# Attention with a block beside it: three pairs of PSUM banks from step 67, and another order of the units

## The chip, the cores and the metric

The kernel runs on one core of one Trainium2 chip. The metric is the device time of one execution in microseconds. One execution was taken by the hardware profiler; all instruction times below come from it. Engines are called as in the profile: PE (matrix multiply; PEld is its weight load), DVE (vector), ACT (scalar), POOL (GpSimd), and SP, which here only issues DMAs. PSUM, where PE writes its results, has eight banks of 512 fp32 columns in each partition as the kernel divides it.

## The reference

One transformer block on x of shape (1, 2048, 448), fp32: layer norm with a shift and scale from a condition vector c, attention with 16 heads of 28, a gated residual, a second such norm, a mixer MLP with 1792 hidden units, a gated residual.

```python
def _A_ref(x, wqkv, wo):
    B, S, D = x.shape
    H = 16; Dh = D // H
    qkv = (lambda x, *d: x.transpose(*d))((x @ wqkv).reshape(B, S, 3, H, Dh), 2, 0, 3, 1, 4)
    q, k, v = qkv[0], qkv[1], qkv[2]
    scale = Dh ** -0.5
    scores = jnp.einsum("bhqd,bhkd->bhqk", q, k) * scale
    p = _softmax(scores, axis=-1)
    o = jnp.einsum("bhqk,bhkd->bhqd", p, v)
    return (lambda x, *d: x.transpose(*d))(o, 0, 2, 1, 3).reshape(B, S, D) @ wo
...
mod = (_silu(c) @ w_mod).reshape(c.shape[0], 6, 1, -1)
sa, ca, ga, sb, cb, gb = (mod[:, 0], mod[:, 1], mod[:, 2], mod[:, 3], mod[:, 4], mod[:, 5])
h = _layernorm(x, axis=-1) * (1 + ca) + sa
x = x + ga * _A_ref(h, A_wqkv, A_wo)
h = _layernorm(x, axis=-1) * (1 + cb) + sb
x = x + gb * _B_ref(h, B_w1, B_b1, B_w2, B_b2)
```

The softmax needs, for each head and query, the largest score, so that the exponentials don't overflow. The kernel computes these maxima by matmuls of their own.

## The kernel before

**Three phases.** Phase 1 (up to about 182 us) makes q, k and v in 512-token blocks and stores q and k, split in a high and a low part for precision, in DRAM. The attention follows (to about 843 us), then the MLP. The change concerns the attention.

**Units and steps.** The 16 heads form four groups g of four heads; the four heads lie in the four 32-row strips of the PE array, 28 rows of data each and a 29th row that carries, on the side of k, a one and, on the side of q, the negated maximum. The queries form four blocks qt of 512. A unit is one (g, qt); there are 16, g outermost: (0,0), (0,1), ... (3,3). A unit has 16 steps kt, one for each 128 keys: 256 steps in all, numbered `step = u * NKT + kt`. A step does in this order:

- the scores of its 128 keys for heads 0 and 1 of the group (`hf` 0, array rows 0 to 63), six matmuls (three terms high × high, low × high, high × low for each of two heads) into a tile of two banks (`ps_s2`, two such tiles), L1051; then the same for heads 2 and 3 (`hf` 1, rows 64 to 127);
- after each half one exponential on ACT of the whole two-bank tile (L1059), into SBUF tiles `slot_c` and `slot_d`;
- between the score matmuls three or four **maxima matmuls** (L392), each one strip of 32 rows against 512 keys into one of three single banks (`ps_mx`), each followed by a DVE reduction over the 512 columns (L397) into `mxp`;
- the product of the previous step's exponentials with v (`av`, L1015), in one bank `o`.

So PSUM is three banks `mx`, two times two banks `s` and one `o`.

**The queue of maxima.** A unit needs 64 maxima: four 128-query tiles i, four heads j, four key blocks cch. They must all be done before the unit's scores start. `queue_max` sorts them by g, then by qt; `emit_max` takes the next that fits the half of the array which the scores leave free. `n_maxima` gives 4 and 3 in turn, and few in steps with output-projection work. `count` reloads a key block (`kh`) or query block (`qh`) for the next g as soon as its last reader is issued (`load_hi`, SP). Phase 1 already does some maxima of later groups. `finish_max` at step kt = 10 makes sure that the next unit's are done; `max_fin` and `put` then negate, transpose and send them by four small DMAs into the 29th rows of the unit's q tile. When no maxima are left, `share(1, 3)` gives a third score tile.

**Loads.** `load_k` brings the next group's keys (four chunks of two 256 KB parts) during the last unit of a group, after the step that read the chunk last; `load_q` brings a unit's queries.

**End of a unit.** `unit_end_tasks` spreads over the steps of the next unit: the denominators (L767 to L776, through DRAM), the division on POOL (L781), the split in high and low (L791, L792). A unit whose g isn't the last for its qt stores this to DRAM. The last unit of a qt loads what the others stored (`load_o`) and does the output projection in four tasks `t_wo`, one in each of the steps kt 8 to 11 of the next unit: 12 matmul terms (9 where three groups take part) of 128 rows × 448 columns into an `mx` bank, an ACT copy (L812) and a POOL addition. So projections run in units 12, 13, 14 and 15. The last group of the last block is left to the MLP phase.

## Time and profile before

| | us |
|---|---|
| median of 3 runs | 1141.04 (1140.98 to 1141.12) |
| the profiled execution | 1142.17 |
| its span, first to last instruction | 1140.4 |
| PE busy | 1127.8 |
| DVE busy | 831.6 |
| ACT busy | 683.4 |
| attention, first exponential to the start of the last step's | 184.15 to 842.27 |
| granted PE clock, mean | 0.998 |

Here are a few rows of the view by line (line, engine, operation, output and inputs with partitions × elements, count; busy time and mean duration of one in ns; idle time of the engine just before them and what ended it):

```profile
L1051 PE MATMUL s<-slot_b,slot_a 32*128 32x512 f32 x3072 | 376.0, 420 | 1.6 <-ACT full L812 0.7 <-ACT v L376 0.6 <-ACT slot_c L1059 0.3
L1059 ACT ACTIVATE slot_c<-s 128x1024 f32<-128x1024 f32 x341 | 339.5, 1022 | 77.1 <-PE s L1051 76.7
L1051 PEld LDWEIGHTS s<-slot_b,slot_a 32*128 32x128 f32 x3072 | 211.9, 183 | 250.2 <-ACT slot_c L1059 147.9 <-ACT slot_d L1059 74.8 <-issue 9.1
L392 PE MATMUL mx<-kh,qh 32*128 32x512 f32 x899 | 290.1, 469 | 0.3
```

Busy time is the union of what runs: 3072 score matmuls of 420 ns fill 376.0 us because up to four run side by side in their strips. In the views by stretch of time a row gives the stretch, its length, then for each engine its busy time with the count of instructions, then the granted clock, the DMA engines' mean busy share and GB/s. In the timeline a row gives start, duration, engine, line, operation, output and inputs, the count of merged instructions, and in brackets the idle time before and what ended it. A matmul's duration reaches to its modelled end.

### The profile page before, as it was taken

To read this page: it belongs to the slowest core of one execution; us is meant where nothing else is said; L and a number is where in the kernel's file an instruction comes from. 1 tells how busy PE (TensorE), PEld (TensorE's weight loads), DVE (VectorE), ACT (ScalarE), POOL (GpSimd) and SP (SyncE) were. 2 spreads that over 40 slices of the span, in tenths; PEclk is the share of its full clock that TensorE was granted. 3 is DMA by queue.
4 is the path that set the end of the run, shared out by engine and by line. 5 is a ranking of instruction groups with operands and counts; after the bars stand their busy time and mean duration, and the time that the engine had idled before them with its cause. 6 is when DMAs were issued, how large, how long until landed. Compare 5 with 4: busy or idle time off the path is not lost.

```text
span 1140.4 us, 20798 instructions
## 1 busy us (share of the span) xinstructions
PE 1127.8 (99%) x8380; PEld 678.4 (59%) x8380; DVE 831.6 (73%) x1487; ACT 683.4 (60%) x839; POOL 245.9 (22%) x277
## 2 busy tenths in 40 slices
PE   8999999999999999999999999999999999999998
PEld 6767765444444444444444444545468888888887
DVE  6868787999999999999999977493648853444322
ACT  4655757878878887888788877586762321211110
POOL 2634431211011011101110121214514503123000
PEclk9999999999999999999999999999999999999999
DMA  9543345121222111222211212022113100000000
GB/s 299 194 144 125 111 160 156 38 62 44 67 84 75 53 45 39 76 76 66 66 30 58 89 63 76 10 85 85 53 55 87 43 34 1 1 33 1 33 1 33
DMA packets 50296, 81.12 MB, mean 71 GB/s; under 512 B 12308, under 2 KB 21592, under 8 KB 50200
## 3 DMA queue, kind: packets, MB, share of 16 engines
q1 hardware_dynamic: 44536, 74.83, 20.8%
q0 software_dynamic: 5376, 4.51, 1.5%
q8 instruction: 66, 1.08, 0.4%
q10 hardware_dynamic: 288, 0.46, 0.1%
q14 instruction: 30, 0.25, 0.1%
HBM read 53.11 MB, written 26.35 MB: 70 GB/s over the span
## 4 chain that ended last, share of the span: by engine, by line
PE 95%; DVE 1%; ACT 1%; DMA 1%; issue 1%; POOL 0%; DVEq 0%; ACTq 0%; POOLq 0%
PE s L1051 27%; PE o L1015 22%; PE mx L317 16%; PE pa L339 7%; PE mx L392 7%; PE s L1112 4%; PE s L1113 4%; PE s L1111 4%; PE pa L317 3%; DMA slot_c<-in_w_mod_dram 1%; PE o L240 1%; PE mx L240 1%; PE o L547 0%; ACT slot_c L1059 0%; DMA acc<-in_A_x_dram 0%
## 5 line engine op out<-in xcount | busy, mean ns | idle before, releaser
L397 DVE TENSOR_REDUCE mxp<-mx 128x1 f32<-128x512 f32 x919 | 580.3, 684 | 102.0 <-PE mx L392 95.2
L1059 ACT ACTIVATE slot_c<-s 128x1024 f32<-128x1024 f32 x341 | 339.5, 1022 | 77.1 <-PE s L1051 76.7
L1051 PE MATMUL s<-slot_b,slot_a 32*128 32x512 f32 x3072 | 376.0, 420 | 1.6 <-ACT full L812 0.7
L1051 PEld LDWEIGHTS s<-slot_b,slot_a 32*128 32x128 f32 x3072 | 211.9, 183 | 250.2 <-ACT slot_c L1059 147.9
L392 PE MATMUL mx<-kh,qh 32*128 32x512 f32 x899 | 290.1, 469 | 0.3
L1015 PE MATMUL o<-slot_c,v 128*32 128x512 f32 x1364 | 270.5, 605 | 0.5 <-ACT osb L983 0.4
L1059 ACT ACTIVATE slot_d<-s 128x1024 f32<-128x1024 f32 x171 | 174.7, 1022 | 38.4 <-PE s L1051 38.1
L1015 PE MATMUL o<-slot_d,v 128*32 128x512 f32 x684 | 179.9, 605 | 0.0
L1095 ACT ACTIVATE full<-mx,b_col 128x512 f32<-128x512 f32 x56 | 38.5, 688 | 192.2 <-PE mx L317 180.1
L392 PEld LDWEIGHTS mx<-kh,qh 32*128 32x128 f32 x899 | 115.3, 182 | 7.5 <-DVE mxp L397 1.9
L1098 DVE CAST hi<-full 128x512 fp32r<-128x512 f32 x56 | 25.2, 450 | 129.3 <-ACT full L1095 129.3
L1015 PEld LDWEIGHTS o<-slot_c,v 128*32 128x32 f32 x1364 | 38.0, 108 | 54.9 <-issue 50.1
L317 PE MATMUL mx<-y,slot_a 128*128 128x512 f32 x160 | 60.6, 395 | 0.0
L767 POOL DMA_DIRECT2D den<-osb x16 | 11.4, 716 | 192.5 <-ACT osb L983 192.5
L405 ACT ACTIVATE slot_d<-mx 128x512 f32<-128x512 f32 x48 | 27.0, 597 | 40.0 <-PE mx L392 39.8
L1099 DVE TENSOR_TENSOR lo<-full,hi 128x512 fp32r<-128x512 f32 x56 | 44.1, 788 | 5.6 <-PE mx L240 0.5
L317 PE MATMUL mx<-y,slot_c 128*128 128x512 f32 x152 | 47.5, 396 | 0.1
L1113 PE MATMUL s<-slot_v,lo 128*128 128x448 f32 x128 | 46.7, 365 | 0.0
L1111 PE MATMUL s<-slot_v,hi 128*128 128x448 f32 x128 | 46.6, 364 | 0.0
L1015 PEld LDWEIGHTS o<-slot_d,v 128*32 128x32 f32 x684 | 24.6, 108 | 27.3 <-issue 25.1
L774 POOL DMA_DIRECT2D drec<-den x16 | 9.3, 578 | 145.1 <-DVE den L772 145.1
L317 PE MATMUL mx<-y,slot_v 128*128 128x512 f32 x112 | 39.2, 396 | 0.0
(223 smaller groups left out, 1484.3 us busy)
## 6 DMA issues: line engine op xcount, KB each, us to landing
d<-lo SPq DMA_DIRECT2D x32, 256.0 KB
slot_b<-d SPq DMA_DIRECT2D x32, 256.0 KB
slot_a<-d SPq DMA_DIRECT2D x32, 256.0 KB
d<-hi SPq DMA_DIRECT2D x20, 256.0 KB
osb<-drec POOLq DMA_DIRECT2D x16, 256.0 KB, 5.2
out_dram<-xn SPq DMA_DIRECT2D x16, 224.0 KB
slot_v<-in_w_mod_dram SPq DMA_DIRECT2D x4, 784.0 KB
raw<-in_B_w_dram SPq DMA_DIRECT2D x14, 224.0 KB
```

Source lines behind the costliest of these rows:

```text
L317: pe.matmul(p, a, b, start=(i == 0), stop=(i == len(terms) - 1))
L339: pe.matmul(p, *ts[i], start=(i == 0), stop=(i == len(ts) - 1))
L392: pe.matmul(m, qh_sb[(g, qt)][js, i * 128 : (i + 1) * 128], k[js, :], start=True, stop=True)
L397: dve.tensor_reduce(out=mxp[(g, qt)][:, i, j, cch : cch + 1], in_=m, op=ALU.max, axis=AX.X)
L1015: pe.matmul(o[32 * j : 32 * j + 32, :], v_sb[kt // 4][:, kt % 4, 4 * g + j, :], p[j // 2][:, j % 2, :], start=(kt == 0), stop=(kt == NKT - 1),
L1051: pe.matmul(s2[:, jj, :], ks[rows_, kp, kc], qs[rows_, qp, :], start=(term == 0), stop=(term == 2))
L1059: act.activation(pt[hf], s2, AF.Exp, scale=SCALE)
L1095: act.activation(gf, p, AF.Gelu_apprx_tanh, bias=b1_col[:, i : i + 1])
L1099: dve.tensor_tensor(out=glo, in0=gf, in1=f(ghi), op=ALU.subtract)
L1111: pe.matmul(pp, ghi[:, ts], w_hi, start=(m == 0), stop=False)
L1112: pe.matmul(pp, ghi[:, ts], w_lo, start=False, stop=False)
L1113: pe.matmul(pp, glo[:, ts], w_hi, start=False, stop=(m == NFT - 1))
```

## The change

Four things change in the attention.

- **Order of units.** The first four units stay, (0,0) to (0,3). The others run block by block: (1,0), (2,0), (3,0), (1,1) and so on. From unit 4 on each unit has another group than the next, so keys are loaded during each of units 3 to 14, and the maxima's key blocks follow the order of the queue. Query blocks for the maxima have four slots by unit number. Projections now run in units 7, 10 and 13 (12 terms, kt 10 to 13) and 15 (9 terms, kt 8 to 11); their loads start four steps later, except for unit 15.
- **Banks.** As soon as three maxima per step (eight in a projection step) are enough up to the deadline of every unit (`room`; this is so from step 67), `share(1, 0)` leaves one single bank, and the six others form three pairs, `pairs`. In a step the first half of the scores takes `pairs[0]`, the second `pairs[1]`, two maxima `pairs[2]`; then `pairs[1]` and `pairs[2]` change places. When no maxima are left the three pairs rotate among the scores.
- **Maxima.** Each step has a single (`emit_one`) after the first half's matmuls, in the strips of the second half, and two (`emit_two`) of adjacent heads with one reduction over [128, 2, 512] after the second half, in the strips of the first half. On odd steps the halves change order. In a projection step five more are issued after the fifth term: two pairs and a single; the projection writes into one of the pairs.
- **Deadline.** `finish_max` moves from kt 10 to kt 12.

```diff
+UNITS = [(0, qt) for qt in range(NB)] + [(g, qt) for qt in range(NB) for g in range(1, NG)]
+UNIT_NO = {unit: u for u, unit in enumerate(UNITS)}
...
+    def ps_pair(i):
+        return psp[0].tile([128, 2, 512], F32, tag=f"pair{i}", name=nm("pair"), bufs=1)
...
-    def mm_acc(p, terms):
-        for i, (a, b) in enumerate(terms):
-            pe.matmul(p, a, b, start=(i == 0), stop=(i == len(terms) - 1))
+    def mm_acc(p, terms, done=0, mid=None):
+        for i in range(done, len(terms)):
+            if i == 5 and mid:
+                mid()
+            pe.matmul(p, *terms[i], start=(i == 0), stop=(i == len(terms) - 1))
...
-        tg = ("kh" if kind else "qh") + str(b)
+        tg = f"kh{b}" if kind else f"qh{UNIT_NO[(g, b)] % 4}"
...
-        mxq.sort(key=lambda m: (m[:2] != (0, 0), -m[0] if phase1[0] else m[0], m[1:]))
+        mxq.sort(key=lambda m: (m[:2] != (0, 0), -m[0], m[1:]) if phase1[0] else (UNIT_NO[m[:2]], m[2:]))
...
+        if not phase1[0]:
+            for cch in cchs:
+                run = runs[cch]
+                run[0][1] -= 1
+                if run[0][1] == 0:
+                    run.pop(0)
+                    if run:
+                        load_hi(1, run[0][0], cch)
...
+    def load_next_q(u):
+        if u + 4 < len(UNITS):
+            load_hi(0, *UNITS[u + 4])
...
+    def take(half):
+        fits = [x for x, m in enumerate(mxq[:32]) if m[4] // 2 == half]
+        alone = [x for x in fits if mxq[x][:4] + (mxq[x][4] ^ 1,) not in mxq]
+        return mxq.pop((alone or fits or [0])[0])
+
+    def emit_two(half, t):
+        for x, m in enumerate(mxq[:32]):
+            if m[4] == 2 * half and m[:4] + (m[4] + 1,) in mxq[:40]:
+                g, qt, cch, i, j = m
+                mxq.remove(m)
+                mxq.remove(m[:4] + (j + 1,))
+                for y in range(2):
+                    max_mm(g, qt, i, j + y, kh_sb[(g, cch)], lambda: t[:, y, :])
+                dve.tensor_reduce(out=mxp[(g, qt)][:, i, j : j + 2, cch], in_=t, op=ALU.max, axis=AX.X)
+                count(g, qt, [cch, cch])
+                return
+        two = [take(half) for _ in range(min(2, len(mxq)))]
+        for y, (g, qt, cch, i, j) in enumerate(two):
+            max_mm(g, qt, i, j, kh_sb[(g, cch)], lambda: t[:, y, :])
+        for y, (g, qt, cch, i, j) in enumerate(two):
+            dve.tensor_reduce(out=mxp[(g, qt)][:, i, j, cch : cch + 1], in_=t[:, y, :], op=ALU.max, axis=AX.X)
+            count(g, qt, [cch])
+
+    def emit_one(half):
+        if mxq:
+            m = take(half)
+            max_one(*m)
+            count(*m[:2], [m[2]])
...
-                p = ps_mx()
+                p, spare = wo_banks()
...
-        d_rec, d_split = (4, 8) if staged else (1, 4) if u == NU - 1 else (2, 5)
+        d_rec, d_split, d_wo = (4, 8, 0) if staged else (1, 4, 7) if u == NU - 1 else (2, 5, 7) if u == NU - 2 else (2, 5, 9)
...
-            tasks.append((0, lambda: load_o(qt)))
+            tasks.append((0 if u == NU - 2 else 4, lambda: load_o(qt)))
...
+    def room(s_):
+        need = 0
+        for u in range(s_ // NKT, NU):
+            need += left.get(UNITS[u], 64)
+            if need > sum(8 if is_wo(x) else 3 for x in range(s_, finish_step(u))):
+                return False
+        return True
+
+    def finish_step(u):
+        return NKT * u - 4
+
+    def wo_banks():
+        if not mxq:
+            return ps_mx(), None
+        first, g_, b_ = pairs
+        t = ps_pair(first)
+        pairs[:] = [g_, b_, first]
+
+        def spare():
+            for x, i in enumerate((g_, b_)):
+                if mxq:
+                    emit_two(x, ps_pair(i))
+            emit_one(0)
+
+        return t[:, 0, :], spare
...
-            if not (three or mxq or late):
-                three = True
-                share(1, 3)
+            if not pairs and room(step):
+                pairs = [0, 1, 2]
+                share(1, 0)
...
-            for hf in range(2):
-                s2 = ps_s2()
+            halves = (1, 0) if pairs and step % 2 else (0, 1)
+            for x, hf in enumerate(halves):
+                s2 = ps_pair(pairs[x]) if pairs else ps_s2()
...
+                if pairs and x == 0 and not (step and is_wo(step - 1)):
+                    emit_one(halves[1])
+                if x == 1:
                     p_next = p_tile()
                     pt.append(p_next[:, 0:2, :])
-                act.activation(pt[hf], s2, AF.Exp, scale=SCALE)
+                act.activation(pt[x], s2, AF.Exp, scale=SCALE)
+            if mxq and pairs:
+                emit_two(halves[0], ps_pair(pairs[2]))
+                if step and is_wo(step - 1):
+                    emit_one(halves[1])
+                pairs = [pairs[0], pairs[2], pairs[1]]
+            elif pairs:
+                pairs = [pairs[2], pairs[0], pairs[1]]
+            pt = [pt[halves[0]], pt[halves[1]]]
...
-            if qt == NB - 1 and kt % 4 == 3 and g + 1 < NG:
-                load_k(g + 1, kt // 4)
+            if g_next != g and kt % 4 == 3:
+                load_k(g_next, kt // 4)
```

More of the change, by code (lines that the diff above doesn't have):

```diff
@@ L694, in tile_adaln_block @@
     phase1[0] = False
-    for item in deferred:
-        load_hi(*item)
     for g in range(1, NG):
@@ L936, in w2_item @@
         return ld, go
-    NU = NG * NB
+    NU = len(UNITS)
     sched = {}
```

75 lines of the change are left out of this document (33 added, 42 removed).

## The prediction

> **What bounds the kernel now.** I read the page's busy times first, then three views of the attention stage, which the change touches, by themselves: the exponentials counted by stretch, all engines by stretch, and the timeline.
>
> ```profile
> PE 1127.8 (99%) x8380; PEld 678.4 (59%) x8380; DVE 831.6 (73%) x1487; ACT 683.4 (60%) x839; POOL 245.9 (22%) x277
> ```
>
> PE's 99% doesn't say that PE is the limit: up to four 32-row matmuls run beside each other and all count as one busy stretch. So the stage has to be cut into steps. A step makes two exponentials (L1059). Counted by stretch, then all engines in the middle stretch:
>
> ```profile
> 183.00:348.59 165.59, 129.93 (x134) 1.00 0.23 68
> 348.60:790.60 442.00, 327.79 (x338) 1.00 0.19 57
> ...
> 348.60:790.60 442.00, 441.32 (x4084) 205.19 (x4084) 368.00 (x619) 339.75 (x360) 63.89 (x76) 1.00 0.19 57
> ```
>
> 134 exponentials are 67 steps, so step 67 starts its first one at 348.60; 338 more are 169 steps, so step 236 begins at 790.65. These 169 steps, 67 to 235, take **442.05 us** and are all that the change makes different. Twelve of them hold output-projection work.
>
> ```profile
> 270.05 1.94 ACT L1059 ACTIVATE slot_c<-s 128x1024 f32<-128x1024 f32 x2 [0.80 <-PE s L1051]
> ...
> 271.20 0.49 PE L1051 MATMUL s<-slot_b,slot_a 32*128 32x512 f32 x2
> ...
> 271.21 0.51 PE L392 MATMUL mx<-kh,qh 32*128 32x512 f32 x2
> ...
> 271.54 1.01 PE L1051 MATMUL s<-slot_b,slot_a 32*128 32x512 f32 x6
> 271.77 1.89 DVE L397 TENSOR_REDUCE mxp<-mx 128x1 f32<-128x512 f32 x3 [0.20 <-PE mx L392]
> 272.04 0.18 PEld L1051 LDWEIGHTS s<-slot_b,slot_a 32*128 32x128 f32 x2 [0.32 <-ACT slot_c L1059]
> ...
> 272.21 1.03 ACT L1059 ACTIVATE slot_c<-s 128x1024 f32<-128x1024 f32 x1 [0.22 <-PE s L1051]
> ...
> 272.95 1.06 PE L1015 MATMUL o<-slot_c,v 128*32 128x512 f32 x8
> 273.13 1.02 ACT L1059 ACTIVATE slot_d<-s 128x1024 f32<-128x1024 f32 x1
> ...
> 273.94 0.50 PE L1051 MATMUL s<-slot_b,slot_a 32*128 32x512 f32 x2
> ```
>
> This is a step with four maxima, on the timeline. Scores start at 271.20. The second half of them starts only at 272.04, when the exponential begun before (270.05 + 1.94 = 271.99) has freed its two banks. The product with v follows from 272.95 to 273.94 (1.00). So the scores took 1.75 us instead of what a step with three maxima needs:
>
> ```profile
> 278.96 0.49 PE L1051 MATMUL s<-slot_b,slot_a 32*128 32x512 f32 x2
> ...
> 279.76 0.39 PE L392 MATMUL mx<-kh,qh 32*128 32x512 f32 x2
> 279.80 0.40 PE L1051 MATMUL s<-slot_b,slot_a 32*128 32x512 f32 x2
> 280.12 1.06 PE L1015 MATMUL o<-slot_c,v 128*32 128x512 f32 x8
> ```
>
> Here the scores take 1.16 (278.96 to 280.12); with v's product as above a step is **2.16**. The two kinds alternate, 2.74 and 2.16, so 2.45 on average. The bound is a wait in a ring of buffers: scores with two buffers must wait for ACT, while ACT itself has gaps (0.80 and 0.22 above). Without maxima and with a third score buffer it looks like this:
>
> ```profile
> 802.08 0.98 PE L1051 MATMUL s<-slot_b,slot_a 32*128 32x512 f32 x12
> ...
> 802.99 0.62 PE L1015 MATMUL o<-slot_d,v 128*32 128x512 f32 x2
> ...
> 803.09 2.93 ACT L1059 ACTIVATE slot_c<-s 128x1024 f32<-128x1024 f32 x3 [0.21 <-PE s L1051]
> ```
>
> Both halves run together (other rows of the array), 0.91 from first score to v's product, and the first exponential starts 1.01 after the first score.
>
> **The change part by part.** *How many maxima.* The view by line, DVE alone, over the stage:
>
> ```profile
> L397 DVE TENSOR_REDUCE mxp<-mx 128x1 f32<-128x512 f32 x802 | 505.0, 684 | 76.4 <-PE mx L392 69.6 <-PE s L1051 4.5
> ```
>
> 802 maxima; the first 67 steps, unchanged, emit 4 and 3 in turn: 235. The other 567 are just 3 × 169 + 5 × 12, the new code's three per step and five more inside each of the twelve projection steps. So the maxima still end at step 235, as pairs 157 + 36 = 193 reduces and 181 singles. From 236 on all is as before, but one thing below.
>
> *A plain step.* The six banks now turn: the first half's pair waits for the exponential before it; the second half's pair was the maxima's pair of the step before, so **its wait moves from ACT to DVE**; the maxima's pair waits for the step before's second exponential. The price of the new reduce, 128x1024, is in no row. Nearest are two reads of PSUM on DVE:
>
> ```profile
> L1117 DVE TENSOR_TENSOR xn<-s,acc 128x448 f32<-128x448 f32 x16 | 9.0, 617 | 4.3 <-PE s L1113 4.1
> ```
>
> From 448 to 512 elements (617 to 684) an element costs 1.05 ns, so 1024 take 684 + 536 = **1.22 us**. From below: ACT's 1.02 for the same shape; from above: two singles, 1.37. I take 1.22.
>
> Count from a step's first score. The pair's matmuls are the fourth round, done at 1.20 (280.15 − 278.96); the reduce starts 0.05 later (271.72 to 271.77), ends at 2.47, and the next step's second half may start at 2.52. From there 0.91 to v's product (272.04 to 272.95; the same as both halves together) and 1.00 for it: the step after next begins at 4.43, so two steps take 4.43, one 2.22. DVE has other work in this loop: of its 368.00 us in the stretch, 567 maxima at 505.0/802 = 0.63 take 357, and 11 are left, 0.065 per step. It has 2.22 − 1.17 − 0.63 = 0.42 free per step (the pair's 1.22 less the 0.05 by which a single's 0.68 overlaps the next), so I let half of it count: 0.03. **2.25 per plain step.** Does the rest keep up? The second exponential starts at 1.01 + 0.92 (272.21 to 273.13) and ends at 2.95, so 0.70 into the next step, where the pair's matmul wants it at 0.80: covered by 0.1. Single reduces run from 0.55 (matmul 0.50, start 0.05) to 1.18, before the pair's. The single's bank is free by then. Behind the waiting second half stand, in PE's order, the pair's matmuls and v's product, and ACT's second exponential needs it: those are the 0.91 and the 1.01 counted here.
>
> *A projection step* (rows of one with twelve terms):
>
> ```profile
> 722.93 0.88 PE L317 MATMUL mx<-slot_e,slot_a2h 128*128 128x448 f32 x3
> ...
> 725.26 0.36 PE L317 MATMUL mx<-slot_e,lo 128*128 128x448 f32 x1
> ...
> 725.55 0.50 PE L1051 MATMUL s<-slot_b,slot_a 32*128 32x512 f32 x2
> ```
>
> Twelve terms take 2.62, 0.20 each at the same pace. Five maxima after the fifth term cost two changes of tile shape and two rounds: 0.29 (725.26 to 725.55) + 0.34 (271.20 to 271.54) + 0.32 (279.80 to 280.12) − 0.20 = 0.75, so 3.37. DVE reduces pair, pair, single there; the second pair ends at 0.80 + 0.29 + 0.50 + 0.05 + 1.17 + 1.22 = 4.03, and the next step's second half waits for it until 0.71 into that step (4.08 − 3.37). Together 0.71 + 0.91 + 1.00 + 3.37 = **6.0**. Without that wait it is 5.5 (1.16 + 1.00 + 3.37); with the single's reduce, 0.63, waited for as well, 6.6.
>
> *Order of units.* Key chunks (512 KB) are now fetched per unit, eight units more than before, and the 256 KB key blocks for the maxima likewise: some 25 MB more. They are issued on SP after the last reader, 12 steps (27 us) or more before use. In a burst the queue moved 362 GB/s, so 2 MB need about 6 us:
>
> ```profile
> 705.00:707.00 2.00, 2.00 (x24) 1.12 (x21) 1.74 (x3) 1.79 (x3) 0.00 (x0) 1.00 1.02 362
> ```
>
> So a projection's 1.5 MB load, now five steps ahead (11 us), also fits; a unit's 4 MB in 36 us is a third of this rate. Cost 0; without that cover a chunk that waits for those before it in SP's queue would come up to those 6 us late per unit. The other thing on SP is the small row of maxima, four DMAs per unit:
>
> ```profile
> 716.01 2.24 SPq L439 DMA_DIRECT2D slot_b<-full  x4
> ```
>
> A unit's maxima now may end four steps before it starts and not six. For the last unit they do: the row is sent at step 237 and read at 240, three steps of 2.0 us, in which 2.24 of issue and a landing (no row of it here) fit; I keep 1 us for it below. The projections move to units 7, 10 and 13, and the nine-term one to unit 15, past step 236: 4 × 3 × 0.20 = 2.4 saved there.
>
> *Sum.* 157 × 2.25 + 12 × 6.0 = 353.3 + 72.0; and 4 for the change of pools at step 67 (1), the single held by its one bank in the step after each series (3 × 0.6), and the last row of maxima (1). 429.3 against 442.05 is −12.8, with −2.4 **−15.2**. The profiled execution (1142.17, of which the span is 1140.4) would become 1127.0; the median, 1141.04, becomes **1125.8; I say 1126**.
>
> **The rivals.**
>
> *PE is the floor.* The three-maxima step of before needs 2.16 with no wait. If the reduce is near 1.02 us, two steps take 0.20 less, 2.15 each, and projection steps 5.6: 337.6 + 67.2 + 4 = 408.8, −33.2 − 2.4: **1105**. For it: ACT's row; against: DVE's slope.
>
> *The wait on DVE is longer than the one on ACT (slower).* Its place is the second half's first weight load. Each 0.1 us by which the pair's reduce ends later costs 0.05 per step, 7.9 us in all. The forecast's gain is gone at a step of (442.05 + 2.4 − 72 − 4) / 157 = 2.35, a reduce ending 0.2 later than at 2.47. At 0.38 later (a pair of 1.60 us, or one queued behind a stalled cast) a step is 2.44: 383.1 + 76 = 459.1, +17.1 − 2.4: **1156**. For it: DVE's queue is in order; against: the slope of the two rows.
>
> *Score halves don't overlap.* If PE starts matmuls in program order only, the second half comes after the first, and a plain step is six rounds (the first 0.34, the last 0.32 to v's product, 0.91 − 0.34 − 0.32 = 0.25 between): 0.34 + 4 × 0.25 + 0.32 + 1.00 = 2.66, so 157 × 0.41 = 64 more: **1190**. The twelve score matmuls at 802.08 speak against it: in that order, with one round shared, they would take 0.34 + 3 × 0.25 + 0.32 = 1.41 to v's product, and 0.91 was measured. The Trainium skill, TensorE: Matmul & The Clock Gate, section "The mechanism", says that matmuls start and end in program order without reordering; by that rule this rival would hold, and the row differs.
>
> *It doesn't do what it says.* Where two maxima of a pair aren't both in the queue's window, two single reduces follow each other, 0.63 + 0.68 = 1.31 instead of 1.22: 0.04 per step, 6 us: **1132**. So most of what I expect comes from the turning banks, little from the wide operation.
>
> **How the numbers follow.** The forecast (2.19 to 2.30 per step, 1115 to 1135) has 0.60; the floor 0.15; separate reduces 0.06; slower by the wait on DVE 0.12, a smaller form of it that ends near no change 0.05; no overlap 0.02. The bounds: all low, 157 × 2.15 + 12 × 5.5 + 2 = 405.6, gives 1102; all high, the reduce at 1.37 (2.325 per step), 6.6 and 6, gives 450.2 and 1147. The range, **1104 to 1143**, holds the floor and leaves out about half of the high corner and the slower cases. Within 0.2% (2.3 us, about what a measurement of this kernel can tell from no change) 0.07, slower by more 0.14, faster by more 0.79.
>
> **What would show it.** The new reduce at 1.15 to 1.25 us, 193 of them; first exponentials 2.25 apart from step 67 to 235 in place of 2.74 and 2.16; the second half's weight load waiting 0.3 us, now for the reduce and no longer for ACT; projection steps of about 6.0; step 236 some 13 us earlier than at 790.65; no wait of scores for a DMA. Wrong: a reduce above 1.4 us, steps at 2.35 or more, or key chunks waited for at unit starts.

## The result and the profile after

The changed kernel takes **1183.16 us** (median of four runs, 1181.17 to 1185.17) beside 1141.08 of the kernel before on the same chip: a ratio of **1.0367**, 95% interval 1.0348 to 1.0385. The forecast was 1126, the range 1104 to 1143. It is slower, and by more than the slower rival (1156). The profiled execution took 1181.17 with a span of 1179.4.

The page of the changed kernel, its busy time and DMA totals:

```profile
PE 1154.2 (98%) x8380; PEld 690.0 (59%) x8380; DVE 819.1 (69%) x1297; ACT 683.2 (58%) x839; POOL 245.6 (21%) x277
...
DMA packets 65416, 108.66 MB, mean 92 GB/s; under 512 B 13988, under 2 KB 23272, under 8 KB 65320
```

The same line of the page before:

```profile
DMA packets 50296, 81.12 MB, mean 71 GB/s; under 512 B 12308, under 2 KB 21592, under 8 KB 50200
```

27.5 MB more are moved, where the forecast had said 25. The attention by stretch, all engines; the stretch from step 67 to step 236:

```profile
...
349.92:831.16 481.24, 469.58 (x4095) 219.62 (x4096) 356.80 (x427) 339.58 (x360) 63.48 (x76) 0.98 0.35 104
```

The stretch that the change touches takes **481.24 us** in place of 442.05, with 429.3 forecast. The miss is there, 52 us of it. PE's idle time in it went from 0.7 (442.00 − 441.32) to 11.7 us (481.24 − 469.58), and the mean granted clock from 1.00 to 0.98. DVE in that stretch, by line:

```profile
L533 DVE TENSOR_REDUCE mxp<-pair 128x2 f32<-128x1024 f32 x190 | 230.4, 1218 | 24.3 <-PE pair L399 13.6 <-PE pair L1109 9.9
L404 DVE TENSOR_REDUCE mxp<-mx 128x1 f32<-128x512 f32 x183 | 126.1, 689 | 83.8 <-PE pair L1109 80.9 <-PE pair L399 1.5 <-PE mx L399 1.3
L836 DVE CAST hi<-osb 128x512 fp32r<-128x512 f32 x11 | 4.7, 424 | 16.9 <-POOL osb L826 16.9
```

The reader is to see three things. The wide reduce is 1.218 us, as forecast. The single reduces stand idle for 83.8 us, and what ends nearly all of that is a **score** matmul (L1109), not the maxima matmul whose bank they read (L399). And a cast of 0.42 us stands 16.9 us in DVE's queue, waiting for POOL. Here is a plain pair of steps on the timeline (first scores at 402.20, 404.66 and 407.01):

```profile
402.20 0.50 PE L1109 MATMUL pair<-slot_b,slot_a 32*128 32x512 f32 x2
...
402.22 0.50 PE L399 MATMUL mx<-kh,qh 32*128 32x512 f32 x1
...
403.24 0.69 DVE L404 TENSOR_REDUCE mxp<-mx 128x1 f32<-128x512 f32 x1 [0.52 <-PE pair L1109]
...
403.85 1.22 DVE L533 TENSOR_REDUCE mxp<-pair 128x2 f32<-128x1024 f32 x1
...
406.02 1.07 PE L1071 MATMUL o<-slot_c,v 128*32 128x512 f32 x8
...
407.01 0.49 PE L1109 MATMUL pair<-slot_b,slot_a 32*128 32x512 f32 x2
```

The single's matmul starts 0.02 after the step's first scores and is done at 402.72 by its modelled end, ahead of most of the scores that were issued before it. Its reduce starts only at 403.24, which is 1.04 after the step's first score, when the last scores of the first half have ended. So the wide reduce behind it begins at 1.65 and ends at 2.87 (403.85 + 1.22 − 402.20). The forecast had 0.55, 1.25 and 2.47. With the forecast's own next terms, 2.87 + 0.05 + 0.91 + 1.00 = 4.83 for two steps; the row above gives 4.81. A plain step is **2.405**, not 2.25.

The second thing, in unit 7, the first with projections; POOL, SP and DVE on the timeline:

```profile
468.10 0.91 SPq L801 DMA_DIRECT2D slot_a2h<-o  x2
...
469.14 0.57 POOL L819 DMA_DIRECT2D drec<-den  x1 [6.20 <-DVE den L817]
...
474.88 0.70 POOL L821 DMA_DIRECT2D osb<-drec  x1 [5.17 <-issue]
...
480.58 1.26 POOL L826 TENSOR_TENSOR osb<-osb,osb 128x512 f32<-128x512 f32 x1 [5.00 <-DMA slot_a<-d]
481.88 0.43 DVE L836 CAST hi<-osb 128x512 fp32r<-128x512 f32 x1 [3.57 <-POOL osb L826]
```

The reciprocals go to DRAM (L819) and come back as a broadcast (L821); the division (L826) starts at 480.58. The kernel before, in its first unit with projections (12):

```profile
663.89 0.58 POOL L774 DMA_DIRECT2D drec<-den  x1 [6.23 <-DVE den L772]
666.14 0.70 POOL L776 DMA_DIRECT2D osb<-drec  x1 [1.67 <-issue]
671.05 1.27 POOL L781 TENSOR_TENSOR osb<-osb,osb 128x512 f32<-128x512 f32 x1 [4.21 <-DMA osb<-drec]
```

7.16 from the write to the division, in place of 11.44. (The kernel before has late ones too: 8.95 and 8.54 in units 13 and 14, and 10.50 in unit 7, in which the next group's keys were loaded; the cast waits 0.65 us at most there. The bracket of L826 names a key chunk, L616's; what the division reads is the broadcast.) In the changed kernel the cast waits for the division, and behind it wait the reduces, whose banks the scores need. That step is 7.25 us long. Two stretches of 4 us from there on (the columns are those of the stretches above):

```profile
480.00:484.00 4.00, 1.73 (x11) 0.66 (x7) 2.12 (x4) 1.75 (x2) 2.52 (x2) 1.00 0.21 79
484.00:488.00 4.00, 3.91 (x24) 1.50 (x28) 1.86 (x3) 1.02 (x1) 0.00 (x0) 0.58 0.00 0
```

PE is busy for 1.73 of 4.00 us, and in the next 4 us the granted clock is 0.58. The Trainium skill, TensorE: Matmul & The Clock Gate, section "What's actually happening", gives the half clock after an idle window of about 3.4 us. The half clock agrees (0.50 from 485 to 488 us). A whole idle window was not needed here: PE's longest gap in the first row is 1.73 us, from 481.23 to 482.96.

The 52 us, split by the starts of each step's first exponential:

| steps 67 to 235 | forecast us | measured us |
|---|---|---|
| 157 plain steps | 353.3 (2.25 each) | 377.6 (2.405 each) |
| 12 projection steps | 72.0 (6.0 each) | 77.4 (6.18 each without one of 9.40) |
| four long steps above plain (7.25, 9.56 and 7.11 at kt 9 of units 7, 10, 13; 5.73 at kt 12 of unit 8) | 0 | 20.0 |
| all else | 4 | 6.2 |
| sum | 429.3 | 481.2 |

Beside the kernel before, the same stretch reads otherwise: there 157 plain steps took 384.4 (2.45 each, all else included) and the twelve projection steps 57.6 (4.80 each). So the plain steps do get 6.9 us shorter by the change. The projection steps get 19.8 longer, of which 14.4 were forecast, the four long steps add 20.0 and the rest 6.2. The other 2 us of the miss lie outside the stretch: step 67 begins 1.3 later, and what follows step 236 is 1.5 shorter, not 2.4.

### The profile page after: what moved, and what is told of

Same layout as the page of the kernel before. It is cut to its first block, busy times and chain, and to the rows that moved or that the text cites. A ratio compares the mean times of both kernels' runs of the same rounds, so it can differ in the third digit from the quotient of the medians.

```text
span 1179.4 us, 20820 instructions
## 1 busy us (share of the span) xinstructions
PE 1154.2 (98%) x8380; PEld 690.0 (59%) x8380; DVE 819.1 (69%) x1297; ACT 683.2 (58%) x839; POOL 245.6 (21%) x277
## 5 line engine op out<-in xcount | busy, mean ns | idle before, releaser
L404 DVE TENSOR_REDUCE mxp<-mx 128x1 f32<-128x512 f32 x535 | 349.1, 686 | 124.6 <-PE pair L1109 80.9
L1119 ACT ACTIVATE slot_c<-pair 128x1024 f32<-128x1024 f32 x252 | 251.1, 1022 | 72.7 <-PE pair L1109 71.9
L1109 PE MATMUL pair<-slot_b,slot_a 32*128 32x512 f32 x2268 | 281.7, 431 | 3.1 <-DVE mxp L533 2.7
L1109 PEld LDWEIGHTS pair<-slot_b,slot_a 32*128 32x128 f32 x2268 | 170.7, 186 | 177.5 <-ACT slot_c L1119 90.4
L533 DVE TENSOR_REDUCE mxp<-pair 128x2 f32<-128x1024 f32 x190 | 230.4, 1218 | 24.3 <-PE pair L399 13.6
L399 PE MATMUL mx<-kh,qh 32*128 32x512 f32 x515 | 191.3, 479 | 9.1 <-DVE mxp L404 9.0
L1119 ACT ACTIVATE slot_d<-pair 128x1024 f32<-128x1024 f32 x126 | 128.7, 1022 | 32.4 <-PE pair L1109 31.9
L1109 PE MATMUL s<-slot_b,slot_a 32*128 32x512 f32 x804 | 103.1, 426 | 0.9 <-ACT v L383 0.6
L1119 ACT ACTIVATE slot_c<-s 128x1024 f32<-128x1024 f32 x89 | 88.7, 1022 | 24.6 <-PE s L1109 24.6
L1109 PEld LDWEIGHTS s<-slot_b,slot_a 32*128 32x128 f32 x804 | 58.0, 186 | 70.8 <-ACT slot_c L1119 45.2
L399 PEld LDWEIGHTS mx<-kh,qh 32*128 32x128 f32 x515 | 74.6, 184 | 16.8 <-DVE mxp L404 14.3
L399 PE MATMUL pair<-kh,qh 32*128 32x512 f32 x384 | 75.8, 418 | 0.0
L1119 ACT ACTIVATE slot_d<-s 128x1024 f32<-128x1024 f32 x45 | 46.0, 1022 | 10.2 <-PE s L1109 10.2
```

The source lines that it names most:

```text
L399: pe.matmul(m, qh_sb[(g, qt)][js, i * 128 : (i + 1) * 128], k[js, :], start=True, stop=True)
L404: dve.tensor_reduce(out=mxp[(g, qt)][:, i, j, cch : cch + 1], in_=m, op=ALU.max, axis=AX.X)
L533: dve.tensor_reduce(out=mxp[(g, qt)][:, i, j : j + 2, cch], in_=t, op=ALU.max, axis=AX.X)
L1109: pe.matmul(s2[:, jj, :], ks[rows_, kp, kc], qs[rows_, qp, :], start=(term == 0), stop=(term == 2))
L1119: act.activation(pt[x], s2, AF.Exp, scale=SCALE)
```

## The experiments

"Steps" are differences between the starts of first exponentials.

| run | median us | ratio to before, 95% interval |
|---|---|---|
| the changed kernel | 1183.16 | 1.0367 (1.0348 to 1.0385) |
| 1 single early | 1175.24 | 1.0294 (1.0276 to 1.0312) |
| 2 single and pair early | 1173.58 | 1.0277 (1.0260 to 1.0294) |
| 3 projection's load first | 1175.68 | 1.0296 (1.0252 to 1.0340) |
| 4 changed banks, old order | 1153.93 | 1.0108 (1.0090 to 1.0125) |
| 5 single early, pair after four | 1164.35 | 1.0199 (1.0168 to 1.0230) |
| 6 cast two steps later | 1162.32 | 1.0186 (1.0171 to 1.0201) |
| 7 leftovers one step later | 1182.86 | 1.0365 (1.0349 to 1.0380) |
| 8 runs 5, 6 and 7 together | 1137.11 | 0.9971 (0.9957 to 0.9985) |
| 9 the same, last unit's leftovers on time | 1135.94 | 0.9947 (0.9935 to 0.9960) |
| 10 run 9 in the old order | **1130.56** | 0.9904 (0.9890 to 0.9917) |
| 11 new order, old banks | 1163.21 | 1.0185 (1.0170 to 1.0200) |
| 12 wide reduce as two | 1186.79 | 1.0399 (1.0370 to 1.0428) |
| 13 run 11 without the key chunks | 1153.49 | 1.0100 (1.0081 to 1.0119) |
| 14 the changed kernel without the key chunks | 1158.60 | 1.0161 (1.0143 to 1.0179) |

### The plain step: what lets a reduce start

Theory (called ORDER in the expectations): a reduce starts only when PE is done with everything issued ahead of its matmul. Rival (WIDE): the wide reduce and the ring of banks set the step.

**Run 1.** The single is issued after the first two score matmuls instead of after all six of the first half.

```diff
-                if pairs and x == 0 and not (step and is_wo(step - 1)):
-                    emit_one(halves[1])
+                    if pairs and x == 0 and term == 0 and not (step and is_wo(step - 1)):
+                        emit_one(halves[1])
```

> The single maximum is issued after the first two score matmuls of the step and no longer after all six of the first half. Theory ORDER (a reduce may start only when PE has finished all that was issued before its matmul, so a single behind six score matmuls is late by 0.5 us, and the pair's reduce behind it): the single's reduce starts 0.55 after the first score in place of 1.04; the pair's reduce then waits for its own place behind the second half (0.96 + 0.05 + 1.22 + 0.05), so a plain step falls from 2.41 to 2.29, 157 x 0.12 = 19 us: 1164, all in the plain steps. Theory WIDE (the length of the wide reduce and the ring of three pairs set the step, wherever the single stands): 2.41 per step stays, 1183.

On its timeline:

```profile
385.27 0.49 PE L399 MATMUL mx<-kh,qh 32*128 32x512 f32 x1
...
385.84 0.69 DVE L404 TENSOR_REDUCE mxp<-mx 128x1 f32<-128x512 f32 x1 [0.19 <-PE pair L1109]
...
386.07 0.40 PE L399 MATMUL pair<-kh,qh 32*128 32x512 f32 x2
386.28 0.39 PE L1109 MATMUL pair<-slot_b,slot_a 32*128 32x512 f32 x2
...
386.76 1.23 DVE L533 TENSOR_REDUCE mxp<-pair 128x2 f32<-128x1024 f32 x1 [0.22 <-PE pair L1109]
```

The same matmul at the same moment of the step, issued earlier: its reduce now starts 0.57 after the first scores, not 1.04. The plain step is 2.33 throughout. That the theory holds is seen best on the next instruction: the pair's matmuls end at 386.47, but their reduce starts at 386.76, 0.09 after the last two scores (386.67), which were issued before them. So the wide reduce starts 1.49 after the first scores even now, where the forecast had 1.25. 2.33 is a little above the forecast 2.29, and the total gained less than the 19 us expected because other steps grew (below).

**Run 2.** The pair's matmuls as well, after the first two scores of the second half (`x == 1 and term == 0`).

> As the one before, and the pair's two matmuls are issued after the first two score matmuls of the second half and no longer after all six. Theory ORDER: the pair's reduce can start about 1.25 after the step's first score, plain steps reach what was predicted, 2.22 to 2.25, so 157 x 0.17 = 27 us off the changed kernel: 1156; if the pair's wait for the second exponential holds up the rest of the second half, 2.3 and 1165. Theory WIDE: 2.41 and 1183.

```profile
385.03 1.94 ACT L1122 ACTIVATE slot_c<-pair 128x1024 f32<-128x1024 f32 x2 [0.57 <-PE pair L1110]
...
387.02 0.18 PEld L399 LDWEIGHTS pair<-kh,qh 32*128 32x128 f32 x2 [0.29 <-ACT slot_c L1122]
```

The alternative that was written down came true for the step (2.3), while the total stayed above its 1165. The pair's weights wait for the second exponential (385.03 + 1.94 = 386.97, load at 387.02), and the scores issued behind them wait too. Steps are 2.54 and 2.12, again 2.33 on average. So the pair must be issued neither last nor first.

**Run 5.** The single as in run 1, the pair after the fourth score matmul of the second half.

```diff
+                    if x == 1 and term == 1 and mx_step:
+                        emit_two(halves[0], ps_pair(pairs[2]))
...
-            if mxq and pairs:
-                emit_two(halves[0], ps_pair(pairs[2]))
+            if mx_step:
```

> Edit: the single's maxima matmul is issued after the first two score matmuls of a step, the pair's after the fourth score matmul of the second half. By ORDER (a reduce starts only when PE has finished all that was issued ahead of its matmul) the wide reduce starts two score matmuls earlier than in the run with the single early alone, where the step was 2.33 us: the loop on VectorE is worth about 4.2 us for two steps, the one on ScalarE about 4.32, PE's own work about 2.15 a step, so a plain step of about 2.2 us, and 157 x 0.2 = 31 us less than the changed kernel's 1183, that is 1152; if the long steps of the late units grow as they did in the runs with earlier maxima, 1160 to 1170. By WIDE (length of the reduce and its ring set the step) the step stays at 2.33 to 2.41 and the time at 1173 to 1183.

```profile
398.38 0.39 PE L399 MATMUL pair<-kh,qh 32*128 32x512 f32 x2
398.55 0.39 PE L1110 MATMUL pair<-slot_b,slot_a 32*128 32x512 f32 x2
...
398.82 1.23 DVE L533 TENSOR_REDUCE mxp<-pair 128x2 f32<-128x1024 f32 x1
```

Now the reduce starts 0.05 after its own matmuls (398.77) while scores issued later still run (to 398.94). Steps of 2.29, 2.28 and 2.15 follow each other, 2.24 on average: **the step of the forecast**, reached by moving two lines. The total is in the 1160 to 1170 that was written for the case that the long steps grow. ORDER is shown; WIDE falls, since reduce and ring are the same. One rival to ORDER would be that PE reports the single at once, and that its reader only counts reports that scores and maxima share. The trace, which also keeps the times of the semaphore updates, speaks against it. In the changed kernel's step above, the sixth score and the single each update PE's semaphore; the updates come at 403.19 and 403.22, and there is none from 402.1 to 403.18. In the stretch from step 67 to step 236 the first update after a single's modelled end comes 0.47 us later (median of 182 singles); in runs 1 and 5 it comes 0.01 us later. So PE itself reports the single only behind the scores issued ahead of it.

**Run 12.** The wide operation by itself: two reductions of one bank in its place.

```diff
-                dve.tensor_reduce(out=mxp[(g, qt)][:, i, j : j + 2, cch], in_=t, op=ALU.max, axis=AX.X)
+                for y in range(2):
+                    dve.tensor_reduce(out=mxp[(g, qt)][:, i, j + y, cch : cch + 1], in_=t[:, y, :], op=ALU.max, axis=AX.X)
```

> The changed kernel with the reduction over two banks done as two reductions of one bank each. By the loop on VectorE (wide reduce 1.22, two singles one after the other 0.63 + 0.69 = 1.32) the pair's bank comes free 0.10 later, 0.05 per plain step: 2.455 in place of 2.405, 8 us more, 1191 (1187 to 1195). If the length of the reduce isn't on the loop: 1183; if the two short ones are better (the first may start after its own matmul): under 1180.

The two take 1.28 together, 0.06 more than the wide one. Steps are 2.40 and 2.47, 2.435 on average: 0.03 more than 2.405, half of 0.06 as a loop of two steps makes it. The runs lie at 1182.78 to 1193.21, so the total tells it less well than the step. The wide operation is worth about 5 us (157 × 0.03), and the rest of the change had to bring any larger gain, as the prediction said.

### The long steps: what the order of units costs

**Run 4.** The changed banks and maxima with the order of before (g outermost). Pairs then begin at about step 102.

```diff
-UNITS = [(0, qt) for qt in range(NB)] + [(g, qt) for qt in range(NB) for g in range(1, NG)]
+UNITS = [(g, qt) for g in range(NG) for qt in range(NB)]
```

> The units run in the order of before (head group outermost), the banks and the maxima as in the changed kernel. If the banks alone cost: plain steps stay at 2.41, so the kernel stays well above before: about 1160 to 1170, the rest being the long steps that come with the key traffic. If the order of units is the main cost: plain steps near 2.25 and about 1130 to 1145.

29 us less than the changed kernel; the plain step is 2.405 again, as the first alternative has it, but the total lies below its 1160 to 1170. No step of units 7 to 11 is longer than 2.64; unit 12, the first with projections, has two of 8.11 and 9.56 in its projection. So the order costs about 29 us on top of the banks, and the forecast had 0 for it. This is the difference of two whole kernels: the pairs cover 134 steps here and 169 there, and of the 29 us only the 20 of the long steps are traced below.

**Run 11.** The other way round: the new order with the three single banks, two score tiles and single reductions of before all through.

```diff
-            if not pairs and room(step):
-                pairs = [0, 1, 2]
-                share(1, 0)
+            if not three and not mxq and not late:
+                three.append(1)
+                share(1, 3)
...
-        if not mxq:
-            return ps_mx(), None
+        return ps_mx(), None
...
-            n = 4 if plain[0] % 2 else 3
+            n = 2 if is_wo(step) else 4 if plain[0] % 2 else 3
```

> The new order of units with the old banks (three single banks, two score tiles, single reductions, four and three maxima in turn, two in projection steps) through the whole attention. If the order costs by itself (traffic delays the denominators' row, VectorE's cast stands ahead of the reduces): the 29 us between the changed kernel and its old-order form appear here too, 1165 to 1175. If the order is harmless as long as VectorE's reduces aren't the bound (the ring of three single banks and the wait for ScalarE leave it slack): 1141 to 1150, and the cost of the changed kernel is one of order and banks together.

22 us above before, 2 below what the first alternative gave, and three steps hold 19.4 of them: 8.25, 9.36 and 9.10 at kt 8 of units 7, 10 and 13 (26.71 − 3 × 2.45). The first of them:

```profile
479.47 1.25 POOL L826 TENSOR_TENSOR osb<-osb,osb 128x512 f32<-128x512 f32 x1 [4.50 <-DMA osb<-drec]
...
480.76 0.43 DVE L836 CAST hi<-osb 128x512 fp32r<-128x512 f32 x1 [3.33 <-POOL m L435]
...
481.84 0.79 PE L399 MATMUL mx<-kh,qh 32*128 32x512 f32 x1 [3.17 <-DVE mxp L404]
```

Same picture as in the changed kernel: DVE's cast behind POOL's late division, reduces behind the cast, PE behind the reduces for 3.17 us. The order costs this by itself, whatever the banks. (The bracket names another POOL instruction, L435, which ran just before; what the cast reads is L826's output.)

**Run 6.** In the changed kernel the cast alone is issued two steps later.

```diff
-        d_rec, d_split, d_wo = (4, 8, 0) if staged else (1, 4, 7) if u == NU - 1 else (2, 5, 7) if u == NU - 2 else (2, 5, 9)
+        d_rec, d_split, d_wo = (4, 10, 0) if staged else (1, 4, 7) if u == NU - 1 else (2, 5, 7) if u == NU - 2 else (2, 7, 9)
```

> Edit: VectorE's cast of the divided outputs (hi and lo) is issued two steps later in each unit, and nothing else is moved. If the long steps come from VectorE's cast standing in its queue ahead of the reduces while GpSimd's division waits for the denominators, the long steps at the ninth step of units 7, 10 and 13 (7.1 to 9.6 us) and at the twelfth of unit 8 (5.7) go: about -20 us, 1163. The step of 9.4 us in unit 13 stays, and plain steps stay at 2.41. If the long steps have another cause (the clock, a transfer that the scores need), they stay or only move by two steps: 1178 to 1184.

1162.32 for 1163 expected. The four long steps are 2.35, 2.46, 2.45 and 2.38; the 9.4 of unit 13 is 9.11, and a new one of 5.34 ends unit 14 (see run 9). The cast's wait in the stretch falls from 16.9 to 2.0 us:

```profile
L836 DVE CAST hi<-osb 128x512 fp32r<-128x512 f32 x10 | 4.2, 420 | 2.0 <-POOL osb L826 2.0
```

So the wait in DVE's queue is the cause of those 20 us. The division in unit 7 still starts 5.7 us after its broadcast's issue; only DVE no longer stands waiting for it.

**What makes the division late** was tried three times. Run 3 puts the projection's load of 1.5 MB four steps earlier in the program.

```diff
-            tasks.append((0 if u == NU - 2 else 4, lambda: load_o(qt)))
+            tasks.append((0, lambda: load_o(qt)))
```

> The stored outputs for the projection are loaded at the unit's second step again and not at its sixth; the single and the pair stand as in the changed kernel. Theory LOADS (this 1.5 MB burst holds up the denominators' broadcast, POOL's division waits for it, DVE's cast waits for POOL, and the maxima behind the cast): the long steps before the projections (7.25, 9.56 and 7.11 in place of 2.4) go, 15 to 17 us: 1167; plain steps stay at 2.41. Rival KEYS (the key chunks, now fetched in each unit, do it): the long steps stay, 1180 to 1185.

1175.68 lies between the two alternatives, and the four runs spread widely (1168.73 to 1181.16, the profiled one the slowest). The long steps of units 7 and 10 stay (7.43, 9.65) and so does that of unit 8 (5.61); that of unit 13 goes (2.47), but one of 5.85 appears there at kt 5. In unit 7 the load was hardly moved: it is issued at 466.59 in place of 468.10, still just ahead of the reciprocals at 469.13. SP issues in order, and the row of maxima with its wait stands ahead. So unit 7 decides nothing. In unit 10 the load did move, from 0.2 to 7.8 us ahead of the reciprocals, and the division stays late, 13.2 us behind them (13.1 in the changed kernel):

```profile
602.20 0.91 SPq L801 DMA_DIRECT2D slot_a2h<-o  x2
...
609.96 0.58 POOL L819 DMA_DIRECT2D drec<-den  x1 [6.20 <-DVE den L817]
...
614.48 0.70 POOL L821 DMA_DIRECT2D osb<-drec  x1 [3.94 <-issue]
...
623.14 1.26 POOL L826 TENSOR_TENSOR osb<-osb,osb 128x512 f32<-128x512 f32 x1 [7.84 <-DMA osb<-drec]
```

From 613 to 615 the DMA engines moved 4 GB/s, so the load was through before the broadcast was issued. There it is not needed for a late division, which speaks for KEYS; unit 13 speaks for LOADS.

Runs 13 and 14 leave the key chunks out from the fifth unit on, in run 11's kernel and in the changed one; the scores then use keys of an earlier group, and the exponentials' scale is a tenth.

```diff
-                load_k(g_next, kt // 4)
+                if u < 4:
+                    load_k(g_next, kt // 4)
+                else:
+                    kst[(g_next, kt // 4)] = kst[(g, kt // 4)]
...
-                act.activation(pt[x], s2, AF.Exp, scale=SCALE)
+                act.activation(pt[x], s2, AF.Exp, scale=0.1 * SCALE)
```

> The new order of units with the old banks once more, but from the fifth unit on the keys of the next group are not fetched: the scores use the keys that are already there (so these units' scores are not the reference's; the exponentials' scale is a tenth, so that none overflows; instructions and their shapes are the same, 88 DMAs of 256 KB are left out). If the key chunks delay the denominators' way through DRAM, the wait between writing the reciprocals and issuing their broadcast goes back from 3.6 to 6.8 us to about 2.25, the division lands before the cast stands in VectorE's queue, and the steps of 8.25, 9.36 and 9.10 us in units 7, 10 and 13 go: 1163 less 17 to 19, 1144 to 1147. If the projection's load of 1.5 MB or the key blocks of the maxima do it, the three steps stay: 1160 to 1164.

> The changed kernel with the same left out (keys of the next group not fetched from the fifth unit on, scale of the exponentials a tenth). If the key chunks are the cause of the late division: the steps at the ninth place of units 7, 10 and 13 (7.25, 9.56, 7.11) fall to about 2.4 and the one of 5.73 in unit 8 too, some 20 us less, 1160 to 1166, with plain steps at 2.41 and the 9.4 us step of unit 13 as they were. If not: 1178 to 1184.

In run 14 all four long steps go (2.61, 2.47, 2.46 and 2.36; 1158.60, a little below the 1160 to 1166 expected). In run 13 only that of unit 13 goes; those of units 7 and 10 stay, 8.32 and 7.91, and the total is between the two alternatives. Run 14 first, then run 13, unit 7:

```profile
460.72 0.92 SPq L801 DMA_DIRECT2D slot_a2h<-o  x2
...
465.80 0.57 POOL L819 DMA_DIRECT2D drec<-den  x1 [6.21 <-DVE den L817]
...
468.68 0.70 POOL L821 DMA_DIRECT2D osb<-drec  x1 [2.31 <-issue]
```

```profile
464.91 0.91 SPq L801 DMA_DIRECT2D slot_a2h<-o  x2
...
468.85 0.57 POOL L819 DMA_DIRECT2D drec<-den  x1 [6.12 <-DVE den L817]
...
474.79 0.70 POOL L821 DMA_DIRECT2D osb<-drec  x1 [5.37 <-issue]
```

Issued 5.1 us ahead of the reciprocals, the 1.5 MB leave them alone (2.88 from write to broadcast); issued 3.9 us ahead, they cost 5.94. So the expectation of run 13 was too simple. Key chunks are not needed to make the division late: in run 13 a projection's load issued 3.9 us (unit 7) or 1.3 us (unit 10) ahead of the small transfers does it without them. Whether they do it by themselves, run 14 leaves open in unit 7: without them the load too is issued 7.4 us sooner (460.72 for 468.10). Unit 8 has no such load; there the division starts 8.63 us after its broadcast's issue in the changed kernel (536.76 to 545.39) and 6.35 in run 14 (529.30 to 535.65). With unit 10 of run 3, this points to the chunks being enough. What the new order does is put such transfers into every unit and stand them ahead of others in SP's queue. How they slow the small ones down was not tried.

### The 9.4 us step, and the versions that beat both

In unit 13 two maxima are left over at the deadline and go one by one through the lone bank:

```profile
780.12 0.49 PE L399 MATMUL mx<-kh,qh 32*128 32x512 f32 x1 [1.21 <-DVE mxp L404]
...
781.40 0.64 PE L399 MATMUL mx<-kh,qh 32*128 32x512 f32 x1 [0.78 <-DVE mxp L404]
```

**Run 7** moves the deadline of all units by one step, so that one is left.

```diff
-            if u + 1 < NU and step == finish_step(u + 1):
+            if u + 1 < NU and step == finish_step(u + 1) + 1:
```

> Edit: what is left of a unit's maxima is finished one step later, so that one leftover single goes through the lone bank in place of two. Expected: the step of 9.4 us in unit 13 shrinks or goes (some -2 to -7 us with the clock that falls behind it), nothing else changes: 1176 to 1181. If that step isn't from the leftovers, it stays, 1183.

That step shrinks to 7.79, but the total is 1182.86, outside the 1176 to 1181 expected: other long steps are longer in its profiled execution (10.72 in unit 10, 5.72 in unit 9). Right about the step, without effect on the time.

**Run 8** has the edits of runs 5, 6 and 7.

> The three edits together (single after two score matmuls and pair after the fourth of the second half; cast two steps later; leftovers one step later). By ORDER for the plain steps and the queue of VectorE for the long ones: 157 steps of 2.2 us, 12 projection steps of about 6.2 and little else, 420 us for steps 67 to 235 in place of 481: 1120 to 1135, which is below the kernel before. If the long steps have a cause that the cast doesn't carry, 1150 to 1165.

1137.11, just below before and 2 us above the upper end of what was expected. Together the three bring 46 us, alone 19, 21 and 0: a faster plain step makes the late cast cost more, as runs 1, 2 and 5 show (steps of 5.6 to 8.9 at kt 8 of units 7 and 10), so it pays in full only with the cast moved.

**Run 9** takes the last unit out of run 7's edit (`finish_step(u + 1) + (u + 2 < NU)`).

> The three edits together again, but the leftovers of the last unit's maxima are finished at the old deadline. In the run of the three edits the last unit's scores waited 3.6 us for the row of maxima, and its last step before and first step were 5.70 and 3.46 us in place of 2.07 and 2.29. Expected: that wait goes, 4.8 us less, 1132.3 (1131 to 1134). If the wait comes from something else in SP's queue it stays, 1137.

It gained 1.2 us in place of 4.8, and the wait at the last unit stays:

```profile
785.58 0.20 DVE L443 STREAM_TRANSPOSE full<-m 128x32 f32<-128x32 f32 x1
...
789.19 0.32 SPq L841 DMA_DIRECT2D o<-lo  x1
789.60 2.26 SPq L446 DMA_DIRECT2D slot_b<-full  x4
...
793.15 0.98 PE L1110 MATMUL pair<-slot_b,slot_a 32*128 32x512 f32 x12 [3.58 <-DMA slot_b<-full]
```

The row is ready at 785.78 and is issued at 789.60, behind the store of `lo`, which run 6's edit has made later. The second alternative held (1137 expected for it).

**Run 10** is run 9 in the old order.

> The same edits with the old order of units (g outermost); the pairs then begin at about step 102. If the order still costs by its traffic and its long steps: 134 steps of 2.25 in place of 2.405 (-21 us against 1154 of the old order with the changed banks), the leftovers of its first projection unit later (-4 to -6): 1127 to 1130, below the run with the new order. If with the cast moved the order costs nothing any more, its shorter stretch with pairs makes it worse than the new order's 1132 to 1137.

1130.56, the best of all, just above the 1127 to 1130 of the first alternative and 5.4 us below run 9: the order still costs something with the cast moved. DVE from 434 to 773 us:

```profile
L533 DVE TENSOR_REDUCE mxp<-pair 128x2 f32<-128x1024 f32 x148 | 180.7, 1225 | 16.9 <-PE pair L399 11.5 <-PE pair L1110 0.3
L404 DVE TENSOR_REDUCE mxp<-mx 128x1 f32<-128x512 f32 x141 | 97.3, 690 | 30.4 <-PE mx L399 23.1 <-PE pair L1110 5.9
L836 DVE CAST hi<-osb 128x512 fp32r<-128x512 f32 x9 | 3.7, 416 | 0.0
```

The single reduces now wait mostly for their own matmul, and the cast for nothing. It moves the bytes of before. It gains 10.5 us on the kernel before although its twelve projection steps take 69.2 us together, where the kernel before took 57.6.

## Why the prediction was wrong

- **The failed step: when the single's reduce may start.** The prediction has "Single reduces run from 0.55 (matmul 0.50, start 0.05) to 1.18, before the pair's." They run from 1.04 to 1.73, because six score matmuls are issued ahead of the single and the reduce waits for them too. That puts the wide reduce's end at 2.87 in place of 2.47, and the step at 2.405: 157 × 0.155 = 24 us. The same step failed for the pair: once the single is out of the way (run 1), the wide reduce still starts at 1.49 and not at 1.25, behind the last scores. Runs 1 and 5 show both by moving the issue alone, 2.405 to 2.33 to 2.24. The maxima matmul from whose rows the 0.05 was taken (271.21 in the trace of before) is issued directly behind a step's first two scores; behind all six, the 0.05 no longer held.
- **"Cost 0" for the order of units.** Keys are fetched for nine units more than before, not eight (72 more loads of 256 KB), which changes little. The cover that was priced was that of the keys and of the scores, and rightly: the view of waits of the changed kernel has no score matmul that waits for a key chunk. What was not looked at is who else uses those queues: the denominators' way through DRAM, with POOL and DVE's in-order queue behind it. 20 us in the changed kernel (run 6); with the old banks the whole order costs 22 (run 11).
- **The slower rival** had the right place and size (a wait on DVE longer than the one on ACT, the reduce's end 0.38 later for 0.40 measured) and 0.12 of the chance. Its reasons were others: a longer reduce, or one "queued behind a stalled cast". It was queued behind a late single instead, at every step, and the stalled casts came in addition; its 1156 held only the first.
- **Right:** the reduce at 1.22 (1.218), the number of maxima (192 pairs in the stretch, two of them reduced singly, for 193), both halves' scores side by side, 0.91 to v's product and 1.00 for it, and the little worth of the wide operation. Where the reduce may start early, run 5's plain step is 2.24, for 2.25 forecast. The rival without overlap fell.
- **Projection steps**: 6.0 forecast, 6.18 on average without the one of 9.40, which is the leftovers through the lone bank; the prediction did not count them.
- Of the signs that it named for "wrong", one came, steps above 2.35. A reduce above 1.4 us and key chunks waited for did not.

## What to carry to other kernels

When a buffer's release moves from one engine to another, work out when the new releaser may **start**: not from the end of the instruction whose data it reads, but from the end of everything issued ahead of that on its producer (shown here for PE); then issue that instruction as early as its own operands allow and no earlier. An in-order queue that releases buffers should hold nothing that waits for a way through DRAM; put such an instruction later, where its input has surely arrived. And more traffic is priced not by its bytes alone, but by the small transfers that are in flight beside it and by what stands behind it in the issuing queue.

## What the runs showed of the hardware

- PE started the single's matmul (issued seventh) at 402.22, 0.02 after the first scores and before the scores issued third to sixth, but its reader was let go only with those. The Trainium skill, TensorE: Matmul & The Clock Gate, section "The mechanism", has matmuls start and end in program order, so that the end of the last one vouches for all. For the start these rows differ; for what a reader may count on, they agree (1.04 here, 0.57 when it was issued third, and PE's semaphore updates as told under run 5).
- The granted clock fell to 0.50 for some 3 us (0.58 over 4) after 4 us in which PE was busy for 1.73. The step that holds both is 4.85 longer than a plain one (7.25 for 2.40), while PE stood without a matmul for 2.3 us of it; v's product at the half clock took 1.87 (485.24 to 487.11) in place of 1.00. So the stall cost more than its own length.
- A write of the reciprocals and its broadcast took 2.25 us from issue to issue in unit 12 of before, where the last large load had been issued 8 us ahead, and 5.74 in unit 7 of the changed kernel, where one was issued 1 us ahead.
